# A hand-scheduled attention and two-MLP kernel: its order of steps becomes a list in the source

## The chip, the cores and the metric

The kernel runs on one core of one Trainium2 chip. Its time is the device time of an execution in microseconds (us); three runs of the kernel before gave 832.71, 832.86 and 833.62, the median is 832.86. Engines are called by the names of the profile: PE is TensorE (PEld its weight loads, that is, the loads of a matmul's stationary operand), DVE the vector engine, ACT the scalar engine, POOL GpSimd, SP the engine that issues most loads and stores.

## What is computed

```
kv  = einsum('bhsd,bhse->bhde', k, v)          # 4 batches, 8 heads, 576 rows, 64 wide
out = einsum('bhsd,bhde->bhse', q, kv)
out = out / sqrt(mean(out*out, -1) + 1e-6) * g_norm
x   = out as (2304, 512)
x   = x / sqrt(mean(x*x, -1) + 1e-6) * rms_g
x   = (silu(x @ w_gate) * (x @ w_val)) @ w_out  # 512 -> 1536 -> 512
h   = x @ w_in                                  # 512 -> 2048 -> 512
out = where(h > 0, h, exp(min(h, 0)) - 1) @ w_out2
```

Inputs are float32, except that the weights come as 64-bit floats and are turned into float32 on the chip.

## The kernel before

**Tiles.** The 2304 rows are 18 tiles of 128, in five blocks: block 0 has tiles 0 and 1, blocks 1 to 4 have four tiles each. Every product is made of three matmuls (high x high, high x low and low x high parts of the two operands). The first MLP has 12 slices of 128 hidden columns (g, v and o are its gate, value and output weights), the second has 16 (i and p). From slice 2 on, and for the pairs of blocks (1, 2) and (3, 4), seven products do the work of eight (lines 661 and 1077, units "pu" for the hidden products and "pb" for the products back); their sums reuse one accumulator bank, so that a product must be copied out by ACT or taken by DVE before a follower may start in the same bank.

**Stages.** The head (to about 100 us) loads the key/value tiles, sums kv for each batch on PE (sum_kv, line 379), makes attention products (attend, "po", line 418), and takes each tile through a chain: square on ACT, mean and guard on DVE, a wide inversion on POOL (invert, line 445), norm and weigh on DVE, square2 on ACT, a narrow inversion on POOL (invert2, line 463), norm2 on ACT, and, for two tiles together, a transpose on PE ("turn", line 476) that ACT and DVE split into high and low parts. Weights go through eight steps of conversion (line 525), most of them on DVE. Slices 0 and 1 of the first MLP are done plainly while the head runs; the dense part follows. While PE has nothing to do before the last kv sum, short matmuls that do no work (keep_warm, line 371) keep it going; the plan says where.

**What sets the order.** Every step of every engine is declared with plan.add (engine, length, rank, what it must follow, which tile it takes). Plan.run (line 204) first shifts ranks by pseudo-random amounts (moved, line 28, with the list MOVES), then places the steps one by one with the declared lengths and lags (order, line 84), then reorders six times by latest possible time (again and latest), keeps the shortest plan, and issues the instructions in its order. LAG holds, for each engine, how long a result takes to its own and to another engine. The chip keeps each engine's order; real waits are semaphores. All loads of inputs go through SP's queue in the order of LOADS (line 1257); weights and some of q pass through four staging tiles st0, sx0, st1, sx1. Two lines matter for the change:

```
LOADS = [0, "g0", 1, 2, 3, 4, "q0", "gains", "v0", "q1", 5, "o0", 6, 7, 8, "q2"]
LOADS += [9, 10, 11, 12, 13, "q3", 14, 15, "g1", 16, 17, "q4", "v1", "q5", "o1", "q6", "q7", "q8"]
```

A number is a key/value tile, q0 to q8 hold two tiles of q each. Behind them come the other weights, in an order that the change leaves alone.

Of the kernel before, what the change touches and what calls it, by code (L numbers as in the profile page):

```python
# [25 lines left out]


def moved(unit, move):

    h = crc32(f"{move}:{unit}".encode())  # L30
    if h % (4, 16, 64)[move // 4 % 3]:
        return 0.0
    return ((h >> 8) % 2001 - 1000) / 1000.0 * (4, 12, 40, 120)[move % 4]


class Plan:
# [3 lines left out]

    LAG = {"DVE": (0.09, 0.13), "ACT": (0.11, 0.17), "POOL": (0.05, 0.1), "PE": (0.0, 0.15), "DMA": (0.0, 0.1), "ADD": (0.0, 0.1), "NOTE": (0.0, 0.0)}
    PATIENCE = 0.03
# [21 lines left out]
    def reach(self, name, engine):  # L64
        e = self.steps[name]["engine"]
        return self.ends[name] + self.LAG[e][e != engine]

# [72 lines left out]

    def again(self):
# [4 lines left out]
        then = {}  # L146
        for n, xs in after.items():
            for x in xs:
                then.setdefault(x, []).append(n)
        self.ends, self.log = {}, []  # L150
        self.clock = dict(self.start)
        waits = {n: len(xs) for n, xs in after.items()}
        ready = {e: [] for e in self.clock}
        for n, k in waits.items():
            if not k:
                ready[self.steps[n]["engine"]].append((n, 0.0))
        for _ in range(len(self.steps)):
            best = None
            for engine, names in ready.items():
                now = self.clock[engine]  # L160
                here = None
                for n, at in names:
                    at = max(now, at)
                    rank = self.steps[n]["rank"]
                    if here is None or at < here[0] - self.PATIENCE or at <= here[0] + self.PATIENCE and (rank, at) < (here[1], here[0]):
                        here = at, rank, n
                if here and (best is None or here[:2] < best[:2]):
                    best = here
            at, _, n = best
            s = self.steps[n]  # L170
            engine = s["engine"]
            ready[engine] = [x for x in ready[engine] if x[0] != n]
# [3 lines left out]
            for x in then.get(n, ()):  # L176
                waits[x] -= 1
                if not waits[x]:
                    e = self.steps[x]["engine"]
                    ready[e].append((x, max(self.reach(y, e) for y in after[x])))  # L180
        return max(self.ends.values())

    def latest(self):

        need = {n: list(self.then.get(n, ())) for n in self.steps}
        for key, taker in self.rooms:
            for u in self.users[key]:
                need[u].append(taker)
        late, t = {}, 0.0
        for _, n, e, length in self.log:  # L190
            if e == "PE":
                late[n] = t
                t += length
        for _, n, e, length in reversed(self.log):
            s = self.steps[n]
            ends = [late[x] - self.LAG[e][self.steps[x]["engine"] != e] - s["lat"] for x in need[n] if x in late]
            here = min(ends, default=t) - length
            late.setdefault(n, here)
        return late

    PASSES = 6
    FILL, SPACE = 0.225, 0.15

    def run(self):
        self.held, self.start = dict(self.holder), dict(self.clock)
        self.then = {}
        for n, s in self.steps.items():
            for x in s["after"]:
                assert x in self.steps, (n, x)
                self.then.setdefault(x, []).append(n)  # L210
        for n, s in self.steps.items():
            unit = str(n[0] if isinstance(n[0], tuple) else n[:4]).replace(" ", "")
            s["rank"] += sum(moved(unit, m) for m in MOVES)
        end = self.order()
        assert end, "no step can start"
        best = end, self.log
        for _ in range(self.PASSES):
            late = self.latest()
            for n, s in self.steps.items():
                s["rank"] = late[n]  # L220
            end = self.again()
            if end < best[0]:
                best = end, self.log
        self.log = best[1]
# [12 lines left out]

MOVES = (
    92370, 83652, 97420, 4511, 77189, 3136, 20512, 6293, 96268, 46460, 33383, 4281, 84592, 62804, 7872, 29216, 36788, 69466, 96741, 78838, 75196, 40078, 44092, 12272,
)  # L240
# [12 lines left out]
def linear_attention__swiglu__elu_kernel(  # L253
# [22 lines left out]
    W = 4 * P  # L276
# [3 lines left out]
    at = 0  # L280
    while at < NT:
        n = min(4, NT - at) if at else (NT % 4 or 4)
# [221 lines left out]
    EW, EW2, ETS = 0.6, 0.335, 0.335  # L504
    AP_, AS = 0.48, 0.53

# [18 lines left out]
    def conversion(n, rank, after, lone, users, summed=None):  # L525
# [45 lines left out]
        def rest():  # L571
# [7 lines left out]
        seq_ = [  # L579
            (begin, "ACT" if spare else "DVE", AS if spare else ETS, [(c, ("c", n))]), (scale, "DVE", ETS, []), (shift, "DVE", ETS, []),  # L580
            (sign, "DVE", EW, [(c, ("w", n))]), (tail, "ACT" if spare else "DVE", AS if spare else ETS, []),
            (add, "DVE", EW, []), (part, "ACT", AS, [("W", ("h", n))]), (rest, "DVE", EW, [("W", ("l", n))]),
        ]
# [98 lines left out]
    def paired(unit, X, one, two, rank, erank, xdeps, finish):  # L682
# [149 lines left out]
    def back(k, t, rank, erank, es=None):  # L832
# [9 lines left out]
        for e in [j for _, j in back_names(ph, fs[0], t)] if es is None else es:  # L842
# [27 lines left out]
            if not last:  # L870
# [15 lines left out]
                else:  # L886
                    plan.add(("issue", k, t, e), "POOL", 0.95, erank, accumulate, [("dump", k, t, e)])
                    plan.add(
# [188 lines left out]
    def back_halved(k, X, rank):  # L1077
# [82 lines left out]
        for c in range(2):  # L1160
# [10 lines left out]
            if seeded_:  # L1171
# [8 lines left out]

                plan.add((unit, "snap1", c), "ACT", AP_, rank, seed, [(unit, 1, c)])
                plan.add((unit, "total1", c), "ACT", AP_, rank, taken, [(unit, 2, c)], [("P", keys[1])])
# [7 lines left out]
            for j, key in keys.items():  # L1190
                _, _, t, e = key
                if k == 0 or groups[k - 1][0] != ph:
# [7 lines left out]
                plan.add(  # L1200
                    ("issue", k, t, e), "POOL", 0.95, rank,
                    lambda key=key, t=t, e=e: nc.gpsimd.dma_start(out=where(ph, t, e), in_=live.pop(key), accum_op=ALU.add),  # L1202
# [100 lines left out]
    for i in range(NT):  # L1303
# [10 lines left out]
        plan.add(("guard", i), "DVE", 0.08, r, lambda i=i: guard(i), [("mean", i)])  # L1314
        plan.add(("invert", i), "POOL", 1.75, r, lambda i=i: invert(i), [("guard", i)])
        plan.add(("norm", i), "DVE", 0.6, r, lambda i=i: norm(i), [("invert", i)])
        plan.add(("weigh", i), "DVE", 0.6, r, lambda i=i: weigh(i), [("norm", i), ("in", "gains")])
        plan.add(("square2", i), "ACT", 0.63, r, lambda i=i: square2(i), [("weigh", i)])
        plan.add(("invert2", i), "POOL", 0.8, r, lambda i=i: invert2(i), [("square2", i)])
        plan.add(("norm2", i), "ACT", 0.61, r, lambda i=i: norm2(i), [("invert2", i)])  # L1320
# [311 lines left out]
```

## Time and profile before

| | us |
|---|---|
| median of 3 runs | 832.86 |
| profiled execution | 832.97 |
| its span, first to last instruction | 831.0 |
| PE busy | 817.1 |
| PEld busy | 680.7 |
| DVE busy | 743.1 |
| ACT busy | 634.9 |
| POOL busy | 235.2 |

The span is what the trace shows; 832.97 - 831.0 = 1.97 us lie around it. Busy times are sums over instructions of one engine. PE's are modelled at the end, so that a matmul that is followed at once by another overlaps it in the trace.

### The profile page before, as it was taken

Reading aid. Unit: us, or ns where it says so; the run is one execution under the profiler, and the core shown is the slowest. Engines: PE = TensorE matmul, PEld = TensorE weight load, DVE = VectorE, ACT = ScalarE, POOL = GpSimd, SP = SyncE. Lnnn points to the kernel's source line nnn. Section 1 sums busy time; section 2 is a strip of 40 time slices with the busy share of each in tenths; the row PEclk is TensorE's granted clock in tenths of the full one; section 3 lists DMA queues with packets and bytes.
Section 4 is the critical chain, followed back from the end, with each engine's and each line's share of the span. In section 5 each row is a group of like instructions: output and inputs, shape, how many; then the busy total and the mean of one; then the engine's idle time right before and its main releaser. Section 6 shows DMA issues by size and latency. Waiting matters only on the chain.

```text
span 831.0 us, 12552 instructions
## 1 busy us (share of the span) xinstructions
PE 817.1 (98%) x4246; PEld 680.7 (82%) x4246; DVE 743.1 (89%) x1360; ACT 634.9 (76%) x1209; POOL 235.2 (28%) x258
## 2 busy tenths in 40 slices
PE   8999999999999999999999999999999999999998
PEld 7888778888888888888888788887878788788886
DVE  4999898998879878887898999989999999998985
ACT  2898677677777567667655789989899999898982
POOL 2655333023113204204300000043333333334332
PEclk9999999999999999999999999999999999999999
DMA  9952378459639729728942244498998888989898
GB/s 365 373 179 88 89 151 143 113 100 161 140 62 174 150 50 165 141 58 134 179 163 76 79 147 125 124 154 159 133 188 149 135 149 157 169 145 159 127 189 229
DMA packets 56144, 124.06 MB, mean 149 GB/s; under 512 B 6160, under 2 KB 10000, under 8 KB 56080
## 3 DMA queue, kind: packets, MB, share of 16 engines
q0 software_dynamic: 30944, 54.01, 46.4%
q1 hardware_dynamic: 25136, 69.25, 24.1%
q8 instruction: 33, 0.54, 0.3%
q14 instruction: 31, 0.25, 0.1%
HBM read 57.18 MB, written 66.06 MB: 148 GB/s over the span
## 4 chain that ended last, share of the span: by engine, by line
PE 77%; DVE 10%; ACT 5%; issue 3%; DMA 2%; POOL 2%; SPq 1%; DVEq 0%; POOLq 0%; ACTq 0%
PE b L808 9%; PE hid L966 6%; PE b L793 2%; DMA wacc<-in_q 1%; POOL ri L447 1%; DMA raw_o<-in_w_out 1%; POOL ri L465 1%; PE ('pb', 9, 3)_a L1145 1%; PE ('pb', 10, 3)_a L1145 1%; PE ('pu', 0, 3, 1)_a L677 1%; PE ('pb', 7, 3)_a L1145 1%; PE ('pb', 13, 1)_a L1145 1%; PE ('pu', 1, 6, 3)_a L677 1%; PE ('pb', 2, 3)_a L1145 1%; DVE z L450 1%
## 5 line engine op out<-in xcount | busy, mean ns | idle before, releaser
L1202 POOL DMA_DIRECT2D out<-part x104 | 91.3, 938 | 293.3 <-ACT part L1179 165.1
L1202 POOL DMA_DIRECT2D mid<-part x64 | 57.5, 939 | 189.8 <-ACT part L1179 64.6
L1011 ACT ACTIVATE e<-e 128x512 f32<-128x512 f32 (+1 forms) x73 | 45.4, 628 | 0.8
L808 PE MATMUL b<-act,h_o 128*128 128x512 f32 x128 | 40.4, 394 | 0.9 <-DVE act L751 0.6
L880 POOL DMA_DIRECT2D mid<-part x26 | 26.5, 1137 | 51.9 <-ACT part L874 51.3
L874 ACT ACTIVATE part<-b 128x512 f32<-128x512 f32 x66 | 38.9, 599 | 1.6 <-PE b L808 1.0
L447 POOL TENSOR_TENSOR ri<-ms,nhalf 128x8 f32<-128x8 f32 x18 | 34.5, 1921 | 16.1 <-DVE ms L443 15.9
L1109 DVE TENSOR_TENSOR e<-e,e 128x512 f32<-128x512 f32 x56 | 38.4, 685 | 0.2
L808 PEld LDWEIGHTS b<-act,h_o 128*128 128x128 f32 x128 | 23.7, 188 | 7.1 <-DVE act L751 1.5
L808 PE MATMUL b<-act,l_o 128*128 128x512 f32 x64 | 24.9, 390 | 0.0
L808 PE MATMUL b<-h_p,act 128*128 128x512 f32 (+1 forms) x68 | 23.3, 381 | 0.5 <-DVE far L914 0.5
L933 DVE TENSOR_TENSOR far<-far,b 128x512 f32<-128x512 f32 x27 | 18.2, 684 | 4.7 <-PE b L808 4.1
L808 PE MATMUL b<-act,h_p 128*128 128x512 f32 x64 | 19.7, 389 | 0.0
L793 PE MATMUL b<-act,h_o 128*128 128x256 f32 x96 | 18.1, 285 | 0.2 <-DVE act L751 0.2
L966 PE MATMUL hid<-xl,h_i 128*128 128x256 f32 x64 | 18.1, 282 | 0.0
L966 PE MATMUL hid<-xh,l_i 128*128 128x256 f32 x64 | 18.1, 282 | 0.0
L966 PE MATMUL hid<-xh,h_i 128*128 128x256 f32 x64 | 18.0, 281 | 0.0
L465 POOL TENSOR_TENSOR ri<-ms,nhalf 128x1 f32<-128x1 f32 x18 | 14.6, 814 | 11.4 <-ACT junk L461 11.4
L793 PEld LDWEIGHTS b<-act,h_o 128*128 128x128 f32 x96 | 15.5, 191 | 1.1 <-DVE act L751 0.4
L461 ACT ACTIVATE junk<-z 128x513 bf16<-128x513 f32 x18 | 11.6, 642 | 5.9 <-DVE z L456 5.9
L468 ACT ACTIVATE z<-z,ri 128x512 f32<-128x512 f32 x18 | 12.7, 737 | 4.1 <-POOL ri L465 3.9
L808 PEld LDWEIGHTS b<-h_p,act 128*128 128x128 f32 x68 | 12.6, 188 | 3.6 <-DVE far L914 0.7
(2362 smaller groups left out, 3193.8 us busy)
## 6 DMA issues: line engine op xcount, KB each, us to landing
out<-part POOLq DMA_DIRECT2D x116, 256.0 KB, 5.4
mid<-part POOLq DMA_DIRECT2D x90, 256.0 KB, 5.5
raw_i<-in_w_in SPq DMA_DIRECT2D x16, 512.0 KB, 5.2
raw_p<-in_w_out SPq DMA_DIRECT2D x16, 512.0 KB, 4.7
raw_g<-in_w_gate SPq DMA_DIRECT2D x12, 512.0 KB, 3.5
raw_v<-in_w_val SPq DMA_DIRECT2D x12, 512.0 KB, 6.2
raw_o<-in_w_out SPq DMA_DIRECT2D x12, 512.0 KB, 6.7
mid<-part SPq DMA_DIRECT2D x18, 256.0 KB, 2.2
```

The lines of the kernel that those rows point to most:

```text
L447: nc.gpsimd.tensor_tensor(ri, ms_t.pop(i), nhalf, op=ALU.pow)
L465: nc.gpsimd.tensor_tensor(ri2, ms2_t.pop(i), nhalf[:, 0:1], op=ALU.pow)
L793: nc.tensor.matmul(po[:, j * n:(j + 1) * n], l[:, s], r, start=first and i == j == 0, stop=f == fs[-1] and i == 2, skip_group_check=True,)
L808: nc.tensor.matmul(po, l, r, start=first and i == 0 and not half, stop=f == fs[-1] and i == 2, skip_group_check=seeded(ph, k, t) or half i ...
L874: nc.scalar.activation(x, pbank["b", k, t, e][:, :n], AF.Copy)
L880: nc.gpsimd.dma_start(out=where(ph, t, e), in_=flat(live.pop(key), t or ph), accum_op=ALU.add)
L933: nc.vector.tensor_tensor(x, x, pbank["b", k, t, e][:, :n], op=ALU.add)
L966: nc.tensor.matmul(pbank[key][:, j * n:(j + 1) * n], l, r, start=bool(opens) and i == 0, stop=c == KD - 1 and i == 2, skip_group_check=not ...
L1011: nc.scalar.activation(live[key], live[key], AF.Exp, scale=-1.0)
L1109: nc.vector.tensor_tensor(raw(*into), raw(*x), raw(*y), op=ALU.subtract)
L1145: nc.tensor.matmul(pbank[key], l[:, sl], r, start=first and i == 0, stop=i == 2, skip_group_check=True)
L1202: lambda key=key, t=t, e=e: nc.gpsimd.dma_start(out=where(ph, t, e), in_=live.pop(key), accum_op=ALU.add),
```

## The change

Plan.again, latest and the pseudo-random moves go. The list SHIFTS gives rank shifts for single steps by name; order() with them decides only which tile each step takes. The order of all 4,545 steps is then the list ORDER: numbers in the order in which the steps were declared (0 to 191 are the loads in pairs, the issue and the arrival; 192 on are the kv sums, and so forth), with times from the new method timed(), which places only the idle matmuls. In timed() a result on its way into PE or POOL takes another 0.11 or 0.1 us (INTO). Some lengths and lags of the plan change. LOADS has a new order up to q8, and WHOLE_AFTER goes from 15 to 17: the sums of x for the paired products ("whole", line 1493) wait for the last tile's narrow inversion.

```
-    LAG = {"DVE": (0.09, 0.13), ..., "POOL": (0.05, 0.1), "PE": (0.0, 0.15), ...}
+    LAG = {"DVE": (0.09, 0.14), ..., "POOL": (0.05, 0.2), "PE": (0.0, 0.2), ...}
+    INTO = {"PE": 0.11, "POOL": 0.1}
...
+    def lag(self, e, engine):
+        return self.LAG[e][0] if e == engine else self.LAG[e][1] + self.into.get(engine, 0.0)
...
+    def timed(self):
...
+        for i in ORDER:
+            n = names[i]
             s = self.steps[n]
             engine = s["engine"]
+            at = max([self.clock[engine] if engine != "NOTE" else 0.0] + [self.reach(x, engine) for x in after[n]])
             self.ends[n] = at + s["length"] + s["lat"]
             self.clock[engine] = at + s["length"]
...
-            s["rank"] += sum(moved(unit, m) for m in MOVES)
+            s["rank"] += SHIFTS.get(unit, 0)
+        self.into = {}
+        assert self.order(), "no step can start"
+        self.into = self.INTO
+        self.timed()
...
+SHIFTS = {
+    "('go',0)": -166, "('in',0)": -1299, "('go',1)": -9, "('in',1)": -385, "('go',2)": 8, "('in',4)": 28,
...
+ORDER = (
+    0, 2, 1, 4, 3, 5, 192, 193, 6, 194, 8, 7, 195, 10, 9, 196, 198, 197, 12, 14, 11, 220, 16, 15, 490, 230, 221,
...
-WHOLE_AFTER = 15
+WHOLE_AFTER = 17
...
-    AP_, AS = 0.48, 0.53
+    AP_, AS = 0.48, 0.525
...
-            plan.add((unit, "snap", 1), "ACT", AP_, erank, seed, [(unit, 1, 1)])
+            plan.add((unit, "snap", 1), "ACT", 0.515, erank, seed, [(unit, 1, 1)])
...
-        plan.add(("invert2", i), "POOL", 0.8, r, lambda i=i: invert2(i), [("square2", i)])
+        plan.add(("invert2", i), "POOL", 0.6, r, lambda i=i: invert2(i), [("square2", i)])
...
-    LOADS = [0, "g0", 1, 2, 3, 4, "q0", "gains", "v0", "q1", 5, "o0", 6, 7, 8, "q2"]
-    LOADS += [9, 10, 11, 12, 13, "q3", 14, 15, "g1", 16, 17, "q4", "v1", "q5", "o1", "q6", "q7", "q8"]
+    LOADS = [0, 1, 2, 3, 4, 'q0', 'gains', 'g0', 'q1', 5, 6, 7, 8, 'v0', 'q2', 'o0', 'q3', 'q4', 9, 10, 11, 12, 13, 'q5', 'q6', 14, 15, 16, 17, 'g1', 'v1', 'q7', 'o1', 'q8']
```

Put into names, the first steps on PE are these (kv with the batch left out; g, v and b are the hidden and back products of slice 0 for block 0):

```
before: kv 0-4, kv 4, po 0-3, kv 5-8, po 4, kv 9, 10, po 5, kv 11, 12, turn 0a, kv 13, 13, turn 0b, po 6,
        g g, po 7, g, kv 14, g v, kv 15, v v v, turn 1, kv 16, 17, b b, turn 2, po 8-10, block 1: g ...
after:  kv 0-4, po 0, 1, kv 4, po 2, 3, kv 5-8, po 4, turn 0, po 6, 5, g g g g v v v v, kv 9, 10, turn 1b,
        kv 11-13, turn 1a, b, kv 13, b, po 7, kv 14, po 8, kv 15, turn 2a, kv 16, turn 2b, kv 17, po 10, block 1: g, po 9, g ...
```

On POOL the inversions begin 0, 1, 2, narrow 0, 3, narrow 1 before, and 0, 1, 2, 3, narrow 0, narrow 1 after.

## Rows read from the trace of the kernel before

**Rows 1.** Page, section 1: busy us, share of the span, instructions.
```profile
PE 817.1 (98%) x4246; PEld 680.7 (82%) x4246; DVE 743.1 (89%) x1360; ACT 634.9 (76%) x1209; POOL 235.2 (28%) x258
```

**Rows 2.** Busy time by stretch: from:to, length, PE busy, clock, DMA share, GB/s.
```profile
40.00:120.00 80.00, 76.94 (x428) 1.00 0.45 126
120.00:440.00 320.00, 319.51 (x1558) 1.00 0.68 129
440.00:813.00 373.00, 370.97 (x1714) 1.00 0.76 144
```

**Rows 3.** PEld waits, three stretches, first and last: total us, times, longest.
```profile
PEld pt L482 <- ACT z L468: 2.3, 2, 1.3
...
PEld pt L482 <- issue: 0.2, 1, 0.2
PEld ('pb', 5, 3)_a L1145 <- ACT part L1165: 0.7, 1, 0.7
...
PEld ('pb', 4, 3)_c L1145 <- ACT part L1179: 0.2, 1, 0.2
PEld ('pu', 1, 4, 3)_a L677 <- ACT ('pu', 1, 4, 3)_b L695: 1.5, 1, 1.5
...
PEld ('pb', 12, 1)_a L1145 <- DVE ('pb', 12, 1)_s L1098: 0.2, 1, 0.2
```

**Rows 4.** Timeline at 656: start us, us, engine line op out<-in [idle <-releaser].
```profile
656.08 0.62 PE L1145 MATMUL ('pb', 10, 3)_a<-('pb', 10, 3)_s,Sh_p 128*128 128x512 f32 x2
656.54 0.39 PE L1145 MATMUL ('pb', 10, 3)_a<-('pb', 10, 3)_s,Sl_p 128*128 128x512 f32 x1
656.80 0.30 PEld L1145 LDWEIGHTS ('pb', 10, 3)_a<-('pb', 10, 3)_s,Sh_p 128*128 128x128 f32 x2 [0.30 <-ACT part L1165]
656.80 0.73 PE L1145 MATMUL ('pb', 10, 3)_a<-('pb', 10, 3)_s,Sh_p 128*128 128x512 f32 x2
657.37 0.40 PE L1145 MATMUL ('pb', 10, 3)_a<-('pb', 10, 3)_s,Sl_p 128*128 128x512 f32 x1
```

**Rows 5.** Timeline of TensorE at 574.
```profile
574.46 0.50 PE L677 MATMUL ('pu', 1, 4, 3)_a<-T2h,Sh_i 128*128 128x512 f32 x1 [1.10 <-ACT ('pu', 1, 4, 3)_b L695]
```

**Rows 6.** Chain that ended last, two pieces: start us, us, what.
```profile
136.33 1.43 PE hid L966 x12
...
800.67 0.68 PE ('pb', 14, 1)_b L1145 x3
```

**Rows 7.** Timeline of the first 46 us, TensorE and one scalar step.
```profile
8.82 0.69 PE L389 MATMUL kv<-wxl 128*64 128x64 f32 x16 [0.20 <-DMA wxl<-in_kv]
...
10.07 0.69 PE L389 MATMUL kv<-wxl 128*64 128x64 f32 x16 [0.15 <-DMA wxl<-in_kv]
...
13.01 2.02 PE L427 MATMUL po<-kv,wxl 128*128 128x128 f32 x16 [0.27 <-ACT kv L403]
...
25.55 0.71 ACT L468 ACTIVATE z<-z,ri 128x512 f32<-128x512 f32 x1
...
29.31 0.66 PE L482 MATMUL pt<-ident,z 128*128 128x128 f32 x4
...
32.23 0.36 PE L966 MATMUL hid<-xh,h_g 128*128 128x256 f32 x1
...
45.19 0.47 PE L966 MATMUL hid_g<-xh,h_g 128*128 128x512 f32 x1
```

**Rows 8.** Timeline of GpSimd, first three wide inversions.
```profile
16.68 5.57 POOL L447 TENSOR_TENSOR ri<-ms,nhalf 128x8 f32<-128x8 f32 x3 [3.59 <-DVE ms L443]
```

**Rows 9.** Busy by stretch: length, PE, PEld, DVE, ACT, POOL, clock, DMA, GB/s.
```profile
20.00:40.00 20.00, 18.69 (x289) 16.40 (x285) 19.39 (x41) 15.58 (x37) 14.87 (x13) 1.00 1.01 399
...
60.00:80.00 20.00, 18.97 (x118) 16.64 (x117) 19.30 (x42) 17.00 (x40) 13.39 (x11) 1.00 0.26 98
```

**Rows 10.** Timeline of the vector engine: g0's first and last step.
```profile
5.71 0.43 DVE L538 TENSOR_SCALAR c_g<-raw_g 128x512 uint32<-128x512 uint32 x1 [4.72 <-DMA raw_g<-in_w_gate]
...
9.68 0.69 DVE L573 SCALAR_TENSOR_TENSOR l_g<-w_g,h_g 128x512 fp32r<-128x512 f32 x1 [0.70 <-ACT h_g L569]
```

More of the change, by code (lines that the diff above doesn't have):

```diff
@@ L22 @@
 INF_FIELD = 2.0**-96 * 1.75
-from zlib import crc32
[L28 to L33, printed above, removed]
 class Plan:
-    LAG = {"DVE": (0.09, 0.13), "ACT": (0.11, 0.17), "POOL": (0.05, 0.1), "PE": (0.0, 0.15), "DMA": (0.0, 0.1), "ADD": (0.0, 0.1), "NOTE": (0.0, 0.0)}
+    LAG = {"DVE": (0.09, 0.14), "ACT": (0.11, 0.17), "POOL": (0.05, 0.2), "PE": (0.0, 0.2), "DMA": (0.0, 0.1), "ADD": (0.0, 0.1), "NOTE": (0.0, 0.0)}
+    INTO = {"PE": 0.11, "POOL": 0.1}
     PATIENCE = 0.03
@@ L65, in reach @@
         e = self.steps[name]["engine"]
-        return self.ends[name] + self.LAG[e][e != engine]
+        return self.ends[name] + self.lag(e, engine)
+    def lag(self, e, engine):
+        return self.LAG[e][0] if e == engine else self.LAG[e][1] + self.into.get(engine, 0.0)
     def room(self, kind, engine, chosen):
@@ L145, in again @@
             after[taker] += self.users[key]
[L146 to L149, printed above, removed]
+        names = list(self.steps)
+        assert sorted(ORDER) == list(range(len(names)))
         self.ends, self.log = {}, []
         self.clock = dict(self.start)
[L152 to L169, printed above, removed]
+        for i in ORDER:
+            n = names[i]
             s = self.steps[n]
             engine = s["engine"]
-            ready[engine] = [x for x in ready[engine] if x[0] != n]
+            at = max([self.clock[engine] if engine != "NOTE" else 0.0] + [self.reach(x, engine) for x in after[n]])
             self.ends[n] = at + s["length"] + s["lat"]
@@ L175, in again @@
             self.log.append((at, n, engine, s["length"]))
[L176 to L201, printed above, removed]
     FILL, SPACE = 0.225, 0.15
@@ L212, in run @@
             unit = str(n[0] if isinstance(n[0], tuple) else n[:4]).replace(" ", "")
-            s["rank"] += sum(moved(unit, m) for m in MOVES)
[L214 to L224, printed above, removed]
+            s["rank"] += SHIFTS.get(unit, 0)
[3 more added lines that the diff above has]
+        self.timed()
         last, end = 0.0, self.steps[self.filled_until]
@@ L579, in conversion @@
         seq_ = [
-            (begin, "ACT" if spare else "DVE", AS if spare else ETS, [(c, ("c", n))]), (scale, "DVE", ETS, []), (shift, "DVE", ETS, []),
-            (sign, "DVE", EW, [(c, ("w", n))]), (tail, "ACT" if spare else "DVE", AS if spare else ETS, []),
-            (add, "DVE", EW, []), (part, "ACT", AS, [("W", ("h", n))]), (rest, "DVE", EW, [("W", ("l", n))]),
+            (begin, "ACT" if spare else "DVE", 0.565 if spare else 0.37, [(c, ("c", n))]), (scale, "DVE", ETS, []), (shift, "DVE", ETS, []),
+            (sign, "DVE", EW, [(c, ("w", n))]), (tail, "ACT" if spare else "DVE", 0.565 if spare else 0.37, []),
+            (add, "DVE", 0.61, []), (part, "ACT", AS, [("W", ("h", n))]), (rest, "DVE", EW, [("W", ("l", n))]),
         ]
@@ L886, in back @@
                 else:
-                    plan.add(("issue", k, t, e), "POOL", 0.95, erank, accumulate, [("dump", k, t, e)])
+                    plan.add(("issue", k, t, e), "POOL", 0.78, erank, accumulate, [("dump", k, t, e)])
                     plan.add(
@@ L1179, in taken @@
                     nc.scalar.activation(x, pbank[unit, "b", c], AF.Copy)
-                plan.add((unit, "snap1", c), "ACT", AP_, rank, seed, [(unit, 1, c)])
+                plan.add((unit, "snap1", c), "ACT", 0.515, rank, seed, [(unit, 1, c)])
                 plan.add((unit, "total1", c), "ACT", AP_, rank, taken, [(unit, 2, c)], [("P", keys[1])])
@@ L1314, in linear_attention__swiglu__elu_kernel @@
         plan.add(("guard", i), "DVE", 0.08, r, lambda i=i: guard(i), [("mean", i)])
-        plan.add(("invert", i), "POOL", 1.75, r, lambda i=i: invert(i), [("guard", i)])
+        plan.add(("invert", i), "POOL", 1.8, r, lambda i=i: invert(i), [("guard", i)])
         plan.add(("norm", i), "DVE", 0.6, r, lambda i=i: norm(i), [("invert", i)])
         plan.add(("weigh", i), "DVE", 0.6, r, lambda i=i: weigh(i), [("norm", i), ("in", "gains")])
-        plan.add(("square2", i), "ACT", 0.63, r, lambda i=i: square2(i), [("weigh", i)])
-        plan.add(("invert2", i), "POOL", 0.8, r, lambda i=i: invert2(i), [("square2", i)])
+        plan.add(("square2", i), "ACT", 0.63, r, lambda i=i: square2(i), [("weigh", i)], lat=0.2)
+        plan.add(("invert2", i), "POOL", 0.6, r, lambda i=i: invert2(i), [("square2", i)])
         plan.add(("norm2", i), "ACT", 0.61, r, lambda i=i: norm2(i), [("invert2", i)])
```

6 lines of the change are left out of this document (2 added, 4 removed), and 608 rows, old and new, of tables (ORDER, SHIFTS).

## The prediction

> **What bounds the kernel now.** I read the page's first section, then the busy time of TensorE by stretches, then what TensorE's weight loads (PEld) wait for, then single places in the timeline. TensorE is busy for 817.1 of 831.0 us [rows 1]: it sets the time, and the vector engine is next with 743.1. An order can win only where TensorE waits. Between 40 and 813 us, where the dense work lies, the rows show 80.00 - 76.94 = 3.06 us of idle time up to 120 us, 0.49 up to 440 and 2.03 up to 813, together 5.6 us [rows 2].
>
> That is not all. A matmul's end in this trace is modelled, so a short delay of its weight load stays inside "busy". The waits of PEld show the delays: 10 from 40 to 120 us, 6 from 120 to 440, 30 from 440 to 813, 46 in all; the groups give the first and the last line of each stretch [rows 3]. Their price is read at one place. The two matmuls of a product that starts at 656.08 are followed by the next matmul 0.46 us later; the two that start at 656.80, whose load waited 0.30 us for a scalar-engine copy of the bank, are followed after 0.57 us [rows 4]: 0.11 us more, which no idle column shows. The same comes on top of a true stall: at 574.46 TensorE stands 1.10 us for one copy [rows 5], and pays the load behind it. So 46 x 0.11 = 5.1 us hide in the busy time, beside 5.6 us of open idle time: 10.7 us that another order can win in the dense part, without touching the work.
>
> [...]
>
> **The change, part by part.** No instruction of the computation goes or comes. Read as a list of names, the new order has the same 1,246 TensorE, 1,359 vector, 1,188 scalar, 242 GpSimd and 171 load or store steps; only each queue's order differs (a TensorE step moves by 6.5 places on average, 61 at most). The lengths changed in the calls of plan.add and the new lags are numbers of the planner: they cost nothing on the chip.
>
> *Late loads.* The new plan charges a step's result another 0.11 us on its way into TensorE, and the order was searched under that charge. I checked in the two lists where a product follows one that must first be copied out of the same bank, and counted what stands between. Turnarounds with two steps (1.37 us by the 0.68 us of three matmuls, [rows 6]) or less between them are 100 before and 79 after, of 400; the two closest of before, with no step and with one between, are gone. In the halved back products the tightest kind, product 6 to product 5, falls from 26 to 11. So the list does what it says, but doesn't clear everything: two steps are enough when the scalar engine is free (its copy takes 0.6) and not when it is in the middle of another one, and the plan can be wrong about that by a few tenths. Bounds: nothing removed, or all 5.1 us. I take 60%, above the fifth by which the tight places fall, since the plan now sees the rest of them too: -3.0 us.
>
> *Open stalls.* 5.6 us in some eleven places. The one at 574 is the place with no step at all between product 1 and its follower: in the new list two stand there. Bounds: 0 and 5.6. The 3.06 us before 120 us depend on the chain of the attention steps; the later 2.5 on single copies. Half: -2.8 us.
>
> *The head.* g0 moves from second in the load queue to eighth, v0 from ninth to fourteenth, o0 from twelfth to sixteenth. A load of 512 KB takes one slot of 1.25 us: the key/value tiles that TensorE waits for arrive at 8.82 and 10.07 [rows 7]. So tiles 1 to 4 and q0 land one slot sooner, and the first attention product goes from 13.01 to about 11.8. The scalar chain behind it is longer than the list suggests: GpSimd now takes four of the wide inversions in a row, 5.57/3 = 1.86 us each [rows 8], before the first narrow one. With the first from about 15.2 they last to 22.6; two narrow inversions and the scaling add some 2.4, and turn 0 can start at about 25. In before it starts at 29.31, though its input is ready at 25.55 + 0.71 = 26.26: it stands behind key/value tiles that are still in flight [rows 7]. The hidden products of block 0 come at about 28 instead of 32.23. That is no gain of 4 us, since tiles 9 to 13 now follow them. Summing the steps from there, I reach the hidden products of block 1 at 43.0 to 43.6 us with one attention product (0.9) still owed. The lengths are those of rows 7 less the tenth or two by which a group's last matmul overlaps the next (0.65 a tile, 0.9 an attention product, 0.45 a turn), and 1.43 us for 12 narrow matmuls [rows 6], which makes 2.9 for the hidden products of block 0 and 1.4 for its back product. The kernel before reaches block 1's hidden products at 45.19 [rows 7] with none owed. The lead is 45.19 - 0.9 - 43.3 = 1.0 us. I take -1.0; the ends are below, in the rivals: a gain of 2.5 if nothing waits, a loss of 3 if the vector engine falls behind.
>
> *What the later loads push.* Behind g0 in the load queue the tiles gain a slot, and q3 and q4 pass tiles 9 to 13, which lose two. Tiles 14 to 17 come four slots later or less, at about 36 to 40 us, when TensorE has hidden products of block 0 to do. g0, v0, o0 and q3 still share four staging tiles, so q4 can be issued only when g0's bits are taken (about 17 us) and q5 when v0's are (about 25); both are ahead of the loads' arrival, so I cost them at nothing; without that cover it is a slot, 1.25 us.
>
> *WHOLE_AFTER from 15 to 17.* Sixteen vector additions may start only after the last normalization. They are needed at about 130 us; the vector engine does other work meanwhile. Cost 0, between -1 and +1.
>
> Sum against the profiled execution, 832.97 us: -1.0 - 3.0 - 2.8 = -6.8, so 826.2; the median of the runs shown is 0.1 lower, so 826.1.
>
> **The rivals.**
> *More is won.* All late loads (5.1), four fifths of the idle time (4.4) and a head of 2.5 give -12.0: 821.0. For it: the new list was searched over hundreds of single shifts. Against it: 79 tight turnarounds remain, and the vector engine is busy for 19.39 of 20 us from 20 to 40 and 19.30 from 60 to 80 [rows 9], which leaves little to start sooner.
> *It only trades.* The stalls turn up at other places, since what decides a wait of 0.3 us is finer than the plan's lengths, and the vector engine eats the head's gain: 832.4.
> *Slower: the vector engine in the head.* In before the seven vector steps of g0 run from 5.71 to 10.37 in time that the engine has to spare [rows 10]; their lengths add to 0.43 x 4 + 0.69 x 3 = 3.8, or 3.2 at the spacing of a full queue. Now they fall behind 12.7, into the start of the full stretch, and v0's behind 20.8. The attention's first steps come 1.3 earlier, so the engine is 1.9 us behind, and up to 3.2 with a wait for v0. While TensorE has attention and hidden products in hand that is hidden; from the point where turns and normalizations come later than 60 us than they did, TensorE pays it in full. With the dense part unchanged that is 832.9 + 2.1 = 835.0.
>
> **How the numbers follow.** Forecast 826.1, chance 0.62, own range 822.5 to 830; more won 0.16; a trade 0.12; slower 0.10. A measurement of this kernel can tell about 0.2%, 1.7 us, from no change. Faster by more than that: 0.62 + 0.16 = 0.78; within it 0.12; slower 0.10. The range leaves out the slower case (0.10) and the lower half of the case that wins more (0.08), and takes in the trade: 820.0 to 832.8.
>
> **What would show it.** Right: the first matmul of a turn near 25 us, the first hidden products near 28, and those of block 1 near 43; idle time of TensorE from 40 to 813 us near 2.8 instead of 5.6; the list of PEld waits down from 46 to about 20; the stall at 574 us gone. Wrong: PEld waits as many as before at other lines (the trade), or vector-engine steps named as the releaser of turns and of hidden products between 40 and 120 us with more than 3.06 us of idle time there (slower). What would break the sum as a whole is a clock or a load rate other than before's, which nothing in the change touches.

## The result and the profile after

The changed kernel takes 821.21 us (median of 4 runs, 820.98 to 821.70); the kernel before, on the same chip, 832.79 (4 runs). The ratio is 0.986, with a 95% interval from 0.9843 to 0.9877. That is 11.6 us less, where 6.8 were forecast: inside the range, at the place of the rival that wins more. The profiled execution took 821.7 us and has a span of 819.9. Line numbers of the new kernel are higher, since the two lists stand in its source: the paired hidden products are L677 before and L1231 after, the back products of the pairs L1145 and L1699. In the kernels of the experiments they have other numbers again (L700 and L1168), so that the tile names are what to read by.

The page's first section (it answers [rows 1]: busy us, share of the span, instructions), and the busy time by stretch (it answers [rows 2]: length, PE, PEld, DVE, ACT, POOL busy, clock, DMA share, GB/s):

```profile
PE 809.4 (99%) x4228; PEld 683.8 (83%) x4228; DVE 747.7 (91%) x1360; ACT 636.7 (78%) x1209; POOL 230.8 (28%) x258
```

```profile
40.00:120.00 80.00, 80.00 (x486) 68.49 (x482) 78.35 (x155) 64.09 (x138) 35.40 (x34) 1.00 0.47 129
120.00:440.00 320.00, 320.00 (x1565) 270.24 (x1564) 284.11 (x515) 220.43 (x409) 75.42 (x82) 1.00 0.69 131
440.00:801.00 361.00, 361.00 (x1691) 302.26 (x1690) 349.96 (x620) 330.04 (x618) 97.75 (x112) 1.00 0.78 147
```

TensorE does not stand for a moment from 40 to 801 us; before, it stood 5.6 us. And its busy row fell by 7.7 us with no computing matmul less. Of that, 3.5 us are idle matmuls of the head that are no longer issued (the tile pair kv<-ident: 24 records with 5.0 us before, 6 with 1.5 us after); the other 4.2 us are time that sat inside "busy" and is gone, although the half clock told of below makes the head's matmuls longer. The waits of its weight loads from 40 to 813 us (they answer [rows 3], 46 waits in before; total us, times, longest) are 5 in all, none of them in the dense part after 120 us:

```profile
PEld pt L1036 <- ACT z L1022: 0.4, 2, 0.2
PEld kv L943 <- issue: 0.3, 2, 0.2
PEld b L1362 <- issue: 0.2, 1, 0.2
```

The head went differently from what was forecast. The timeline of TensorE (it answers [rows 7]), and the windows of 2 us from 20 to 28 (columns as above; the clock stands behind POOL):

```profile
11.81 2.02 PE L981 MATMUL po<-kv,wxl 128*128 128x128 f32 x16 [0.98 <-ACT kv L957]
...
22.42 2.88 PE L981 MATMUL po<-kv,wacc 128*64 128x128 f32 x16 [1.89 <-DMA wacc<-in_q]
25.23 1.97 PE L1036 MATMUL pt<-ident,z 128*128 128x128 f32 x8
27.00 1.69 PE L981 MATMUL po<-kv,q 128*128 128x128 f32 x8
...
29.33 0.36 PE L1520 MATMUL hid<-xh,h_g 128*128 128x256 f32 x1
...
45.09 0.48 PE L1520 MATMUL hid_g<-xh,h_g 128*128 128x512 f32 x1
```

```profile
20.00:22.00 2.00, 0.54 (x16) 0.40 (x14) 2.00 (x5) 1.92 (x6) 1.77 (x2) 0.87 1.02 406
22.00:24.00 2.00, 1.58 (x11) 1.58 (x12) 2.00 (x6) 1.14 (x4) 2.00 (x3) 0.50 1.04 414
24.00:26.00 2.00, 2.00 (x13) 1.67 (x10) 2.00 (x5) 0.85 (x2) 0.00 (x1) 0.50 1.02 406
26.00:28.00 2.00, 2.00 (x11) 2.00 (x10) 1.49 (x4) 1.60 (x5) 0.00 (x0) 0.50 1.05 410
```

The fifth attention product stands 1.89 us for a tile of q; the granted clock falls in that window and is 0.50 to about 28 us. In this execution the chain is where it was forecast (first product 11.81, first turn 25.23), but what follows is slow: the hidden products of block 0 come at 29.33 and not 28, those of block 1 at 45.09 with an attention product still owed.

**Where the time went.** Two places tell it, the first paired product and the last matmul, and the end of the span behind them. They are, before, at 129.27 and 827.36:

```profile
129.27 0.39 PE L677 MATMUL ('pu', 0, 2, 1)_a<-xh,h_g 128*128 128x512 f32 x1
...
827.36 0.28 PE L808 MATMUL b<-h_p,act 128*128 128x256 f32 x1
```

and after, at 124.21 and 815.48:

```profile
124.21 0.39 PE L1231 MATMUL ('pu', 0, 2, 3)_a<-xh,h_g 128*128 128x512 f32 x1
...
815.48 0.28 PE L1362 MATMUL b<-h_p,act 128*128 128x256 f32 x1
```

The lead is 5.06 us at the first paired product. By the two lists of names the new kernel owes two back products there (2 x 0.68), so 3.7 are earned by then. It is 11.9 at the last matmul: 8.2 more in the dense part. Behind the last matmul the closing stores take 0.8 us longer in this execution (819.9 - 815.8 against 831.0 - 827.6), which leaves 11.1 in the span. That is not of the change: in two further executions of the same kernel, e8 and e12 below, they take 3.5 and 3.4 us, as long as the kernel before's 3.4.

### The profile page after: what moved, and what is told of

The parts are those of the page before. It is cut to its first block, busy times and chain, and to the rows that moved or that the text cites. A ratio compares the mean times of both kernels' runs of the same rounds, so it can differ in the third digit from the quotient of the medians.

```text
span 819.9 us, 12523 instructions
## 1 busy us (share of the span) xinstructions
PE 809.4 (99%) x4228; PEld 683.8 (83%) x4228; DVE 747.7 (91%) x1360; ACT 636.7 (78%) x1209; POOL 230.8 (28%) x258
## 4 chain that ended last, share of the span: by engine, by line
PE 97%; DMA 2%; SPq 0%; DVE 0%; issue 0%
PE b L1362 11%; PE hid L1520 7%; PE hid_g L1520 3%; PE hid_v L1520 3%; PE b L1347 2%; PE po L981 2%; DMA wacc<-in_q 1%; PE pt L1036 1%; DMA wxl<-in_q 1%; PE kv L943 1%; PE ('pu', 0, 10, 3)_a L1231 1%; PE ('pu', 0, 4, 1)_a L1231 1%; PE ('pb', 10, 1)_a L1699 1%; PE ('pu', 0, 11, 3)_a L1231 1%; PE ('pu', 0, 7, 3)_a L1231 1%; PE ('pb', 4, 3)_a L1699 1%
## 5 line engine op out<-in xcount | busy, mean ns | idle before, releaser
L1756 POOL DMA_DIRECT2D out<-part x104 | 91.8, 910 | 163.4 <-DVE part L1723 62.7
L1434 POOL DMA_DIRECT2D out<-part x12 | 11.0, 917 | 125.4 <-DMA out<-part 107.7
L1001 POOL TENSOR_TENSOR ri<-ms,nhalf 128x8 f32<-128x8 f32 x18 | 32.7, 1818 | 11.8 <-DVE ms L997 11.7
L1048 ACT ACTIVATE xh<-pt,gains_sb 128x256 fp32r<-128x256 f32 x36 | 15.7, 480 | 3.8 <-PE pt L1036 3.8
L1520 PE MATMUL hid<-xh,l_i 128*128 128x256 f32 x64 | 18.1, 283 | 0.0
L1520 PE MATMUL hid<-xl,h_i 128*128 128x256 f32 x64 | 18.1, 283 | 0.0
L1046 DVE SCALAR_TENSOR_TENSOR xl<-pt,gains_sb,xh 128x256 fp32r<-128x256 f32 x36 | 15.9, 476 | 1.1 <-ACT xh L1048 1.1
L1019 POOL TENSOR_TENSOR ri<-ms,nhalf 128x1 f32<-128x1 f32 x18 | 11.0, 615 | 19.0 <-ACT junk L1015 18.9
```

Of the source, the lines that this page charges most:

```text
L1001: nc.gpsimd.tensor_tensor(ri, ms_t.pop(i), nhalf, op=ALU.pow)
L1434: nc.gpsimd.dma_start(out=where(ph, t, e), in_=flat(live.pop(key), t or ph), accum_op=ALU.add)
L1520: nc.tensor.matmul(pbank[key][:, j * n:(j + 1) * n], l, r, start=bool(opens) and i == 0, stop=c == KD - 1 and i == 2, skip_group_check=not ...
```

## The experiments

All kernels carry an order written out by hand; ratios are to the kernel before on the same chip, and lines are of one profiled execution of each. A name such as pu(1,4,3) 7 is product 7 of the seven of the unit ('pu', 1, 4, 3), the paired hidden products of slice 4 of the second MLP; the letter behind a unit names one of its tiles.

**The two halves apart.** e1 has the old order and loads up to the first paired product and the new order behind it; e2 the other way round; e5 is e2 with its seam at a place where the two lists are nearly the same.

```
e1: ORDER = before[: first paired product] + the rest in after's order
e2: ORDER = after[: first paired product]  + the rest in before's order
e5: ORDER = after[: third product of ('pu', 0, 4, 1), near 190 us] + the rest in before's order
```

e1: 

> The order of before up to the first paired hidden product (some 125 us), the order of after from there on, with the loads of before. Theory (the gain is made place by place, where TensorE no longer waits): from 120 us on, before idles for 0.49 + 2.03 us and pays 36 late weight loads at 0.11 = 4.0, so this kernel is 6.5 us faster than before, about 826.3. Rival (the new list works only as a whole, its dense part lives on what its head gets ready sooner): less than 2 us faster, 831 or more, with new idle time after 125 us.

e2: 

> The other half: the loads and the order of after up to the first paired hidden product, the order of before from there on. Theory (place by place): before idles for 3.06 us from 40 to 120 and pays 10 late loads there, 1.1; with some 0.4 from the first 40 us that is 4.6 us faster than before, about 828.2, and the stall at 574 us is still there. Rival (only as a whole): 831 or more. Rival (all of the gain comes from the head and the later loads): 822 to 823.

e5: 

> The new order and loads up to the third product of the eighth paired unit (near 190 us; the two lists differ by only 12 steps there, where they differed by far more at 125 us), the order of before behind it. In e2 the lead of about 5 us at 125 us was lost in one wait of 3.9 us at the seam. Theory A (the wait was a matter of the seam: the steps of DVE and ACT that the list of before puts later): the lead survives here, 5 us less than before, and the stalls of before from 440 us on remain: 828.0 where before gives 832.9. Theory B (the dense part of before cannot use the lead, since its DVE or ACT is what sets the pace there): the lead goes again, 832 to 833, with new waits of TensorE for DVE or ACT spread behind 190 us.

e1 took 828.87 us, ratio 0.9947 [0.9932, 0.9962], a gain of 4.4. e2 took 834.13, ratio 1.0008 [0.9998, 1.0018]: no gain. e5 took 830.31, ratio 0.9966 [0.9954, 0.9979], a gain of 2.8, between its two theories. TensorE's waits from 110 us on (total us, times, longest; e5's up to 440 us), first e1, then e2:

```profile
PE ('pu', 0, 2, 1)_a L700 <- ACT part L897: 1.1, 1, 1.1
PE ('pu', 0, 2, 3)_b L700 <- ACT ('pu', 0, 2, 3)_b L718: 0.7, 1, 0.7
...
```

```profile
PE ('pu', 0, 2, 1)_b L700 <- ACT ('pu', 0, 2, 1)_b L718: 3.9, 1, 3.9
PE ('pu', 1, 4, 3)_a L700 <- ACT ('pu', 1, 4, 3)_b L718: 1.1, 1, 1.1
```

The scalar engine in e2, just ahead of that wait:

```profile
126.44 0.63 ACT L1534 ACTIVATE xh<-w 128x512 fp32r<-128x512 f32 x1 [1.36 <-DVE w L1510]
129.82 0.63 ACT L1534 ACTIVATE xh<-w 128x512 fp32r<-128x512 f32 x1 [2.75 <-DVE w L1510]
```

And e5's waits:

```profile
PE b L816 <- DVE part L1192: 0.9, 1, 0.9
PE ('pb', 2, 3)_c L1168 <- DVE ('pb', 2, 3)_s L1121: 0.6, 1, 0.6
PE ('pu', 0, 4, 1)_c L700 <- DVE ('pu', 0, 3, 3)_u L738: 0.2, 1, 0.2
```

e1's 4.4 and the 1.8 us of waits at its seam make 6.2 for the dense part alone; it has no wait of a load and no idle time from 440 to 813. The trace puts it higher: e1 runs from its first paired product to its last matmul in 692.3 us, where the kernel before takes 698.1, and 5.8 with the 1.8 of the seam is 7.6, near the 8.2 of the new kernel; e1's closing stores were 1.2 us longer than before's. In e2 the lead is there (its first paired product starts at 125.10) and one wait of 3.9 us at the seam takes it: ACT stands 1.36 and 2.75 us for vector sums that the old list has ahead of the bank's copy in ACT's queue. From 133.2 to 136.6 us, behind that wait, e2's granted clock is 0.50 as well. In e5 that wait is gone and 1.7 us of waits for the vector engine stand in its place. So in these three a half of the list was not had at its full worth: TensorE's lead was kept only as far as the queues of ACT and DVE had it too.

**One place opened.** The stall of 1.10 us at 574 [rows 5], where a product follows in its bank with nothing between. e4 moves product 1 two steps forward on TensorE; e6 moves its scalar copy too.

```
TensorE, before:    pu(1,4,3) 7, pb(9,1) 1, pu(1,4,3) 1, pu(1,4,3) 6
TensorE, e4 and e6: pu(1,4,3) 1, pu(1,4,3) 7, pb(9,1) 1, pu(1,4,3) 6
ACT, before and e4: relu, copy of pb(9,1) 1, conversion i, exp, copy of pu(1,4,3) 1
ACT, e6:            relu, copy of pu(1,4,3) 1, copy of pb(9,1) 1, conversion i, exp
```

e4: 

> The kernel before with one place changed: the two matmul steps of product 1 of the unit that stalls at 574 us come two steps earlier, so that two steps stand between it and its follower instead of none. Theory (a stall that costs TensorE 1.10 us of idle time and a late load of 0.11 is won in full, as nothing else is late): 1.1 us faster than before, about 831.7, no idle time at 574. Rival (the wait only moves on, to the next copy or to the vector engine): within 0.3 us of before.

e6: 

> e4 with one thing more: the scalar copy of product 1 of that unit goes three places forward in ACT's queue, ahead of the copy of the other unit, the conversion and the exp. Theory A (a place is opened only when the product and its copy both move): the stall at 575 us (1.10 in before, 2.30 in e4) is gone, 1.1 to 1.3 us less than before, 831.7 where before gives 832.9. Theory B (ACT is simply too full there, and any copy put forward delays another that TensorE waits for): as before or slower, with the stall at a neighbour that waits for ACT.

e4 took 835.97 us, ratio 1.0031 [1.0019, 1.0043]; e6 834.09, ratio 1.0009 [1.0000, 1.0018]. Neither gains. Timeline of TensorE and of ACT in e4:

```profile
575.89 0.50 PE L700 MATMUL ('pu', 1, 4, 3)_a<-T2h,Sh_i 128*128 128x512 f32 x1 [2.30 <-ACT ('pu', 1, 4, 3)_b L718]
```

```profile
573.69 0.58 ACT L1198 ACTIVATE ('pb', 9, 1)_b<-('pb', 9, 1)_a 128x512 f32<-128x512 f32 x1 [1.14 <-PE ('pb', 9, 1)_a L1168]
```

and of TensorE and ACT in e6:

```profile
576.86 0.39 PE L989 MATMUL hid<-xh,h_i 128*128 128x256 f32 x1 [0.77 <-ACT h_i L592]
577.84 0.38 PE L989 MATMUL hid<-xh,l_i 128*128 128x256 f32 x1 [0.47 <-DVE l_i L596]
```

```profile
572.89 0.58 ACT L718 ACTIVATE ('pu', 1, 4, 3)_b<-('pu', 1, 4, 3)_a 128x512 f32<-128x512 f32 x1
574.10 0.58 ACT L1198 ACTIVATE ('pb', 9, 1)_b<-('pb', 9, 1)_a 128x512 f32<-128x512 f32 x1 [0.63 <-PE ('pb', 9, 1)_a L1168]
...
576.19 0.62 ACT L592 ACTIVATE h_i<-w_i 128x512 fp32r<-128x512 f32 x1
```

In e4 the copy stands behind the same scalar steps as before, one of which (the copy of pb(9,1) 1) now waits 1.14 us for a product that comes later; the stall grows from 1.10 to 2.30 us. These 1.2 us are what the edit shows. The median lies 2.6 above the kernel before, but e4's six executions fall in two groups, two of 833.93 and 834.34 (mean granted clock 0.999) and four of 835.85 to 836.20 (0.997), and the rest of the 2.6 is not shown to be the edit's. In e6 the copy is early (572.89) and its stall is gone, but ACT then stands 0.63 us for the other product, the weights' high part comes at 576.19, and TensorE waits 0.77 and 0.47 for it and for the low part: 1.24 for 1.10. (e6 and the kernel before also differ by 0.7 us in one wait near 404 us, far from the edit.) What this place costs is a matter of three queues; it wasn't opened from TensorE's side.

**The price of a late load.** A two-step place is one where two steps of TensorE stand between a product and the follower that needs its bank copied out. e7 is the new kernel with 22 of its two-step places made one-step; e8 is the new kernel itself as its measure.

```
after: pu(0,6,1) 6, pb(3,3) 1, pu(0,6,1) 7, pu(0,6,1) 5     (5 follows the copy of 6)
e7:    pu(0,6,1) 6, pb(3,3) 1, pu(0,6,1) 5, pu(0,6,1) 7     (21 more of the kind)
```

e7: 

> The new kernel with 22 places of the dense part (127 to 758 us) made tight: the product that follows a copied-out one moves one TensorE step earlier, so that one step (0.68 us) stands between them and not two (1.37); nothing else moves on any engine. It prices a late load by itself. [...] Theory A (the price of the prediction, 0.11 us of late load inside the busy time, beside what shows as idle): 22 PEld waits or more, busy time up by 22 x 0.11 = 2.4 us, idle up by 0 to 2: 823.6 to 825.5 where the new kernel gives 821.2. Theory B (a late load costs nothing but its open idle time): no more than the idle time that shows. Theory C (places with one step are no worse than with two): 821.2.

e8: 

> The new kernel itself with its order written out and its planner left out, on the same chip as the others and as the measure for them: 821.2 where before gives 832.9, ratio 0.986.

e8 took 821.73 us, ratio 0.9859 [0.9846, 0.9873]; e7 831.15, ratio 0.9979 [0.9969, 0.9988]. So 22 moves on one engine by 0.68 us each give back 9.4 us, four fifths of the whole gain: 0.43 a place. Busy time by stretch in e7 (length, PE, clock, DMA share, GB/s) and the longest of its 31 PEld waits behind 120 us, 13.8 us in sum:

```profile
120.00:440.00 320.00, 319.02 (x1543) 1.00 0.68 130
440.00:800.00 360.00, 359.26 (x1659) 1.00 0.76 141
```

```profile
PEld ('pb', 7, 3)_c L1168 <- ACT part L1202: 0.7, 2, 0.4
PEld ('pu', 1, 0, 3)_a L700 <- ACT ('pu', 1, 0, 3)_u L734: 0.7, 1, 0.7
...
```

One of them, in the place shown above:

```profile
258.06 0.39 PE L1168 MATMUL ('pb', 3, 3)_a<-('pb', 3, 3)_s,l_o 128*128 128x512 f32 x1
258.46 0.30 PEld L700 LDWEIGHTS ('pu', 0, 6, 1)_a<-T,Sh_g 128*128 128x128 f32 x2 [0.43 <-ACT ('pu', 0, 6, 1)_u L734]
258.46 0.72 PE L700 MATMUL ('pu', 0, 6, 1)_a<-T,Sh_g 128*128 128x512 f32 x2
259.02 0.40 PE L700 MATMUL ('pu', 0, 6, 1)_a<-T,Sl_g 128*128 128x512 f32 x1
```

Idle time shows only 0.98 + 0.74 = 1.7 of the 9.0 us by which the span grew; the other 7.3 sit in the busy time. All three theories fall on the size. From 258.06 to 259.02 three matmuls take 0.96 us, where three at the usual spacing of 0.23 take 0.68 (124.21, 124.44 and 124.66 in the new kernel): this wait of 0.43 us cost 0.28. So it is at 65 of the 67 places where a load waits behind 120 us, 36 in the kernel before and 31 in e7: the two spacings around the late load grow by its wait less 0.15 us. The other two stand behind shorter products, of 256 columns, and cost a little more than they waited (in the kernel before 0.76 for 0.69, at 403.33). In the kernel before a copy that waited for its product began 0.04 us after the product's end (at 507.41, behind 507.37), and a load that waited for a copy started 0.05 after the copy's (at 656.80, behind 656.12 + 0.63).

The sums bear the price out as far as waits go. In e7 it makes 13.8 - 31 x 0.15 = 9.1, where the stretch from the first paired product to the last matmul is 10.1 us longer than in e8 (e7's head was a us quicker, with its clock full, and the span grew by less); in the kernel before 12.0 - 36 x 0.15 = 6.6, where the dense part was 8.2 longer. The remainders, 1.0 and 1.6 us, no wait names. The place read for the prediction had the same price: the matmul with the late load started 0.04 us late itself, which the reading of 0.11 left out, so that a wait of 0.30 cost 0.15 [rows 4]. What was wrong was to take that price as one for every length of wait.

That a load may wait some 0.15 us for nothing fits a load that starts ahead of its matmul, and the traces show such loads. In the kernel before the load for the matmul at 656.54 starts at 656.31, 0.23 us ahead of it, while the two matmuls that start at 656.08 (0.62 us) are in flight:

```profile
656.31 0.19 PEld L1145 LDWEIGHTS ('pb', 10, 3)_a<-('pb', 10, 3)_s,Sl_p 128*128 128x128 f32 x1
```

The loads that waited start with their matmuls, at 656.80 there and at 258.46 in e7. Why 0.15 of the 0.23 us are free is not shown.

**Loads and steps apart.** e9 is the kernel before with the new order of loads, e10 the new kernel with the old one; e12 is the new kernel as their measure.

```
e9:  LOADS of after, the order of before        (19 vector and 3 scalar steps shift)
e10: LOADS of before, the order of after        (6 TensorE steps shift)
```

e9: 

> The kernel before with the new order of loads alone; the order of steps on TensorE, ACT and GpSimd stays as in before (19 vector steps and 3 scalar ones shift within their queues where a later tile makes them). It tells how much of the head's gain the loads make by themselves. Theory A (loads and steps belong together: tiles 1 to 4 come a slot sooner, so the first attention product starts near 11.8, but in the old list the first turn stands behind tiles 11 and 12, which now come two slots, 2.5 us, later): 0 to 2.5 us slower than before, 833 to 835.4 where before gives 832.9. Theory B (the earlier key/value tiles are the gain): 1 to 3 us faster, 830 to 832.

e10: 

> The new kernel with the loads in the order of before; every other queue keeps the new order (6 TensorE steps shift). Tile 8, which the fifth attention product waits for, comes two slots (2.5 us) later, the first four tiles one slot. Theory A (the lead hangs on the loads): 2.5 us more than the new kernel, 824.2 where it gives 821.7, with the first paired product at 126.5 and not 124.1. Theory B (the head is set by the chain behind the products, and the lead comes from the order of steps): 821.7 to 822.5.

e12: 

> The new kernel itself once more, on the same chip as e9 to e11 and as the measure for them: 821.7 where before gives 833, ratio 0.986.

e12 took 821.26 us, ratio 0.9858 [0.9844, 0.9873]. e10 took 824.16, ratio 0.9892 [0.9876, 0.9909]: the loads are worth 2.9 us in the new order, as theory A has it. In the profiled pair 1.6 show at the first paired product (126.36 against 124.74), and 1.6 still at the last matmul (817.71 against 816.11); the other 1.5 of that pair are closing stores, which differ between executions of one kernel too, so that 1.6 of the 2.9 are shown to be the loads'. e9 took 840.10, ratio 1.0086 [1.0071, 1.0101]: 7.3 us slower, three times theory A's worst, and its first paired product starts 7.3 late too (136.54). Timeline of the vector engine in e9, and one wait of TensorE (total, times, longest):

```profile
13.30 0.43 DVE L561 TENSOR_SCALAR c_g<-raw_g 128x512 uint32<-128x512 uint32 x1 [12.31 <-DMA raw_g<-in_w_gate]
...
17.26 0.69 DVE L596 SCALAR_TENSOR_TENSOR l_g<-w_g,h_g 128x512 fp32r<-128x512 f32 x1 [0.69 <-ACT h_g L592]
17.88 1.28 DVE L463 TENSOR_REDUCE ms<-z 128x8 f32<-128x512 f32 x2
```

```profile
PE po L450 <- POOL ri L488: 4.9, 1, 4.9
```

The same engine in the new kernel:

```profile
13.33 0.43 DVE L1099 TENSOR_SCALAR c_g<-c_g 128x512 f32<-128x512 f32 x1
13.67 0.68 DVE L994 TENSOR_REDUCE ms<-z 128x8 f32<-128x512 f32 x1
14.27 0.42 DVE L1102 TENSOR_SCALAR c_g<-c_g 128x512 uint32<-128x512 uint32 x1
```

And in the kernel before:

```profile
14.84 0.68 DVE L440 TENSOR_REDUCE ms<-z 128x8 f32<-128x512 f32 x1
```

This is the slower rival of the prediction at work: the conversion of g0, loaded later, holds up the first attention step from 14.84 to 17.88 when the vector engine has it behind all seven steps of the conversion, as before. The new list puts that step (13.67) between two of them. Not all of e9's 7.3 us is the vector engine's by itself: behind the wait of 4.9 us the granted clock is 0.50 from 26.0 to 32.8 us.

**The half clock.** The new plan asks for ten idle matmuls ahead of the fifth attention product, but keep_warm writes them into a batch's kv bank and the kernel has none open there, so none is issued. e3 and e11 write them into the bank of the product that follows.

```
+        elif name[0] == "po":
...
+            ahead[name] = bank(name)
+            nc.tensor.matmul(ahead[name][:, :P], ident, ident, start=True, stop=True)
e3: 4 ahead of product 0, 8 ahead of product 4        e11: 10 ahead of product 4
```

e3: 

> The kernel after, with short idle matmuls before two attention products that wait for loads: 4 before the first, 8 before the fifth, written into the bank that the product takes next (the plan of after asks for idle matmuls there, but the helper that issues them has no bank at that time, and none was issued). Theory (the wait of 1.9 us at 22 us let the granted clock fall to 0.5 from about 21 to 28 us, and the work in it took twice as long): clock 1.00 from 20 to 40 us, the first hidden products at about 28.0 instead of 29.33, 1.2 us faster than after, about 820.0. Rival (the vector engine sets the head): the hidden products come sooner, TensorE waits later, 821.2 as after.

e11: 

> The new kernel with ten idle matmuls ahead of the fifth attention product, as its plan asks, written to that product's own bank, and nothing else (e3 had eight there and four ahead of the first). In the new kernel TensorE waits 1.9 us there and its granted clock is at half from about 21.4 to 28.2 us. Theory A (the half clock costs what the products between take longer): clock 1.0 throughout, hidden products of block 0 at 28 and not 29.3, and with no wait for a store behind it 820.6 where the new kernel gives 821.7. Theory B (the chain of attention steps or a store gives it back): 821.7.

e3 took 822.29 us, ratio 0.9872 [0.9854, 0.9891]; e11 822.35, ratio 0.9867 [0.9853, 0.9882], beside e12's 821.26. Timeline and one window of TensorE in e11 (length, PE, clock, DMA share, GB/s):

```profile
26.40 1.06 PE L457 MATMUL po<-kv,wacc 128*128 128x128 f32 x8
27.21 0.36 PE L996 MATMUL hid<-xh,h_g 128*128 128x256 f32 x1
```

```profile
22.00:24.00 2.00, 2.00 (x23) 1.00 1.05 414
```

In e11 the clock stays at 1.00, and the hidden products of block 0 come at 27.21, 2.1 us sooner than in the new kernel's profile. But the same head without idle matmuls can keep the clock too. In e7, which has the new kernel's first 127 us, TensorE stands as long, and its hidden products come at 27.97, so that 0.8 of the 2.1 is left for the idle matmuls; in e12, the new kernel once more, the clock fell at the first attention product and was full again in the later gap. First e7, then the window of e12 (length, PE, clock, DMA share, GB/s):

```profile
22.95 1.58 PE L450 MATMUL po<-kv,wacc 128*64 128x128 f32 x16 [1.88 <-DMA wacc<-in_q]
```

```profile
22.00:24.00 2.00, 1.05 (x13) 1.00 1.01 404
```

```profile
12.00:14.00 2.00, 1.77 (x8) 0.56 1.02 410
```

One profile of each can't show that the idle matmuls keep the clock. More executions speak for it: the mean granted clock is 0.999 or 1.000 in all eight of e3 and e11, and 0.997 or less in nine of the new kernel's twelve. That the kernel as a whole gains by it is not shown: e11's profiled execution has a span of 818.6 us, e12's 819.8, but the other executions of e11 are no faster than the new kernel's, and the intervals overlap. What takes it back is in part on the record. Near 523 us ACT waits for a store to free its tile, 1.8 us in e3 (TensorE stands 0.8 behind it) and 1.1 in e11, and not at all in the new kernel: an earlier TensorE meets a store that isn't done. Whether the slower executions lose their time there is not shown.

## Why the prediction came out as it did

| step | forecast | trace |
|---|---|---|
| first attention product | 11.8 | 11.81 |
| first turn | 25 | 25.23 |
| hidden products of block 0 | 28 | 29.33 |
| those of block 1, one product owed | 43.0 to 43.6 | 45.09 |
| lead there | +1.0 | 45.19 - 0.9 - 45.09 = -0.8 |
| idle time, 40 to 813 us | 2.8 | none to 801 |
| PEld waits | about 20 | 5 |

**Direction and mechanism: right.** TensorE's open and hidden waits were the reserve, and the list took them. Going by the busy row alone the time could not fall by more than the idle time; the busy row itself fell by 7.7 us, 4.2 of them without the idle matmuls.

**The terms that were mis-sized: late loads (-3.0) and open stalls (-2.8).** Their upper bounds, 5.1 and 5.6, make 10.7, and 12.7 were won behind the start (the lead of 11.9 at the last matmul, and the 0.8 that the start lost): the reserve was read nearly whole. The shares were not. The 60% rested on the count of tight turnarounds, 100 before and 79 after (92 and 72 when counted by the dependencies in the kernels). e7 and e4 show why that is a poor measure: 72 two-step places stand in the new list and none has a late load, 22 of them one step closer cost 9.4 us, and a place opened on TensorE alone got worse, since there it was the copy's place in ACT's queue that decided. The half for the stalls was no reading at all. With both terms in full and the head as measured the sum is +0.8 - 5.1 - 5.6 = -9.9. Each open stall stands at one of the 46 late loads, whose waits so hold both terms. Priced as in e7 they cost 11.2 (18.1 us in sum, less 46 x 0.15), and with them it is -10.4, against -11.9 at the last matmul; the 1.5 between them no wait names.

That the rival with more won put 821.0 is partly luck: it had the late loads and most of the idle time right, but 2.5 of its 12.0 was a gain of the head, which lost 0.8 in the profile.

**The head: right chain, no gain.** The load order did what was forecast up to the turn. Missed was that product 4 now stands at a point where TensorE has nothing else: 1.89 us of wait, and in the profile the granted clock at half from 21.5 to 28.3 us, which lengthens the turn to 1.97 us and the next attention product's eight matmuls to 1.69 (1.06 at the full clock in e11). In two executions with this head in which the clock did not fall ahead of them, block 1's hidden products come at 44.18 (e2) and 44.58 (e7) and not at 45.09: a lead of +0.1 and -0.3 instead of -0.8, and still not the forecast's +1.0. The prediction said that "nothing in the change touches" the clock; but the kernel before has a mean of 0.999 or 1.0, and most executions of the new one 0.997 or less. The lead of 3.7 us at the first paired product comes from 40 to 120 us, not from the start: the 10 late loads there waited 6.1 us, the open 3.06 among them, which at the price of e7 is 4.6, and with 0.8 off for the head 3.8. And the loads are not worth 1.0: in the new order they are worth 2.9 by the medians and 1.6 at the last matmul, in the old one they cost 7.3 (e10, e9).

**The slower rival.** Its mechanism is real: e9, which has it, loses 7.3 us where the rival put 2.1 (the half clock is in the 7.3); the vector engine is now busy for 78.35 of 80 us from 40 to 120, but its own order was changed along with the loads, and TensorE never waits for it there. That part of the diff, 1,359 vector steps in a new order, was in the prediction only as a count.

**Priced at nothing.** Staging tiles: TensorE's waits name no tile of the later q loads (q3 on). WHOLE_AFTER: no wait from 40 to 801 us. Both fit a cost of zero; neither was tried by itself. Nor was the choice of tiles, which SHIFTS changes for most steps along with the order: the experiments move steps with the tiles of one list or the other, so its share in the gain stays open.

## What to carry to other kernels

Read a matmul engine's reserve from the waits of its weight loads, not from its idle time: sum their lengths and take off what each can wait for free (0.15 us here). In this case the new order won all that this gave, and somewhat more; the forecast had taken about half. An order is one thing over all queues: steps, or the loads, moved on one queue alone lost time here (e7, e9, and e10 the other way), and the place of e4 got worse by it. Where a search changes every queue, look at the queue that the moved work falls into, and at each new gap of TensorE, before giving a term a share.

## What had not been expected of the hardware

The granted clock fell in the head after matmuls that had run at 1.00, and not at the same place in each execution of one kernel. In the new kernel's profile it fell by the gap of 1.89 us at 22 us and was 0.50 from 21.5 to 28.3; in e8 it was 0.50 from 22.9 to 26.3; in e12, the same kernel, from 12.2 to 15.6, behind gaps of at most 0.98 us, and 1.00 in the later gap; in e7 and e2, with the same head and gaps of 1.88 and 1.89 us there, it stayed at 1.00. What decides it is open. A fall goes with about 1 us of the kernel's time, by few executions: the three of the new kernel with a mean clock of 0.999 or more took 819.9 to 821.1 us, the nine others 821.0 to 822.2. A weight load that waited cost its wait less about 0.15 us, at 65 of 67 places in two kernels, and most of what e7 lost (7.3 of 9.0 us) stands inside the busy time of the matmuls.
